# The third and fourth matrix products read their moving columns alternately from two halves of the weight rows

## The chip, the cores and the metric

The kernel runs on one core of a Trainium2 chip. The metric is the device time of one execution in microseconds; three executions of the kernel before give the median. The profile comes from a further, profiled execution, and its times are microseconds from the first instruction unless marked ns.

## What is computed

Causal attention feeds a two-layer network with a SiLU, and its output feeds a second two-layer network with a softmax gate and a layer norm. What matters here is the second network:

```
h    = x @ w_in                          # 896 x 768 @ 768 x 1024   third product
e    = exp(h - max(h)); sm = e / (sum(e) + 1e-9)
solu = h * sm
ln   = (solu - mean) / sqrt(var + 1e-6) * g_ln
out  = ln @ w_out                        # 896 x 1024 @ 1024 x 768  fourth product
```

## The kernel before

Tokens are the 896 rows, in NT = 7 tiles of 128. Each operand of the four products is split into a high and a low part of TensorE's one-pass 32-bit type (fp32r), and each product is three matmuls: high by high, high by low, low by high. The weights arrive as 64-bit numbers in chunks of 128 x 384 and are turned into the high and low parts by ScalarE (ACT), VectorE (DVE) and GpSimd (POOL) while TensorE (PE) works; the DMAs are issued by SyncE (SP).

A matmul has a stationary operand, loaded by its own weight-load instruction (PEld), and a moving one, which is streamed column by column. In the first two products (`gemm1`, lines 380 to 382, and `mm2`, lines 508 to 510) the weights are stationary and the activations move, 448 tokens at a time. Their columns are read through

```
def woven(a):
    return a.rearrange("p (z n) -> p n z", z=2)
```

which takes a contiguous row of 448 numbers in the order 0, 224, 1, 225, and so on: by turns from its first and its second half. What writes those rows (`parted`, `two`) puts even tokens in the first half and odd tokens in the second, so that the result comes out in the normal order.

In the third product (`gemm3`, lines 647 to 649) and the fourth (`product`, lines 702 to 704) it is the other way about: 128 tokens are stationary and the weights move. The moving rows are read from end to end: 512 columns of `w3h` or `w3l` in `gemm3`, 384 columns of a block of the fourth weight in `product`. A call of `gemm3` is 2 x 6 x 3 = 36 matmuls, a call of `product` 4 x 3 = 12. There are 7 calls of `gemm3`. There are 26 calls of `product`: token tiles 0, 1 and 2 take four each in `whole`, and tiles 3 to 6 go in two pairs through `pair4`, which uses seven products for the eight blocks of a pair (sums and differences of weight quarters `t1` to `t4`, and of activations `s1` to `s4`, stand in for the eighth).

The order on each engine is that of the code. Behind each `gemm3(t)` stands `chain(t)`: DVE takes the maximum of the tile (line 661), ACT the exponential (662), DVE multiplies (666), ACT squares and subtracts the mean (669, 670). Two helpers fill the time in between: `fill` converts a chunk of the fourth weight, and `turn` and `take` transpose the normalised tile on PE (line 680) into one of two PSUM buffers `tp` and split it from there, ACT making the high part (684) and DVE the low one (685). `pst` has two `tp` buffers, so a third `turn` waits until the first `take` is through; `psh` has two buffers for `h`, so `gemm3(t + 2)` waits for line 669 of `chain(t)`.

After each call of `product` a function `after()` runs the next entry of the table `steps`: `sums4` scales a part of the weights and builds differences (ACT 825, POOL 827 to 830), `split_t` splits them (ACT 836, DVE 837), `pre` transposes and combines the activations of a pair (PE 680, ACT 684 and 845, DVE 685 and 691). Results leave PSUM by ACT (726, 744, 745) or DVE (740) and are stored by SP.

Of the kernel before, what the change touches and what calls it, by code (L numbers as in the profile page):

```python
# [21 lines left out]
KD = DM // 128  # L22
# [3 lines left out]
KF2 = DF2 // 128  # L26
K2 = KF2 // 2
NT = T // 128
CH = 384
# [51 lines left out]
def fused(ctx, tc, qk, vv, w1, w2, w3, w4, gl, out):  # L81
    nc = tc.nc
# [24 lines left out]
    def woven(a):  # L107
        return a.rearrange("p (z n) -> p n z", z=2)

    def parted(a):  # L110
        return a.rearrange("p (n z) -> p z n", z=2)
# [4 lines left out]
    with tc.manual_schedule():  # L116
# [338 lines left out]
        for step in ORDER.split():  # L455
            step, _, n = step.partition("/")
# [99 lines left out]
        w3h = w3p.tile([128, KD * DF2], F32R, name="w3h", tag="h")  # L556
        w3l = w3p.tile([128, KD * DF2], F32R, name="w3l", tag="l")
# [77 lines left out]
        def columns(t):  # L635
            n, b = divmod(t - 1, B)
            o = S - C if t == 0 else b * (S + C) + 128 * n
            return slice(o, o + 128)

        def gemm3(t):  # L640
            ps = psh.tile([128, 2, 512], F32, name="h", tag="h")
            at = columns(t)
            for n in range(2):
                for k in range(KD):
                    o = (n * KD + k) * 512
                    wh, wl = w3h[:, o:o + 512], w3l[:, o:o + 512]
                    nc.tensor.matmul(ps[:, n], yh[:, k, at], wh, start=k == 0, stop=False)  # L647
                    nc.tensor.matmul(ps[:, n], yh[:, k, at], wl, start=False, stop=False)  # L648
                    nc.tensor.matmul(ps[:, n], yl[:, k, at], wh, start=False, stop=k == KD - 1)  # L649
            hps[t] = ps  # L650
# [48 lines left out]
        def product(ps, z, q, first, last):  # L699
            (ah, al), (bh, bl) = aop[z], split[4, q]  # L700
            for k in range(K2):
                nc.tensor.matmul(ps, ah[:, k], bh[:, k], start=first and k == 0, stop=False)  # L702
                nc.tensor.matmul(ps, ah[:, k], bl[:, k], start=False, stop=False)  # L703
                nc.tensor.matmul(ps, al[:, k], bh[:, k], start=False, stop=last and k == K2 - 1)  # L704

        def four():
            r = raw.tile([128, CH, 2], U32, name="o", tag="wr").bitcast(F32).rearrange("p (n c) z -> p n (c z)", n=2)
# [11 lines left out]
        def whole(t, after):  # L719
            o = four()  # L720
            for n in range(2):
                ps = bank()
                for k in (1, 2):
                    product(ps, (t, k), f"{k}{n + 1}", k == 1, k == 2)
                    if k == 2:
                        nc.scalar.activation(o[n], ps, AF.Copy, scale=rstd[t])
                        store(t, n, o[n])
                    after()

        def pair4(g, after):  # L730
# [3 lines left out]
            def made(z, q):  # L734
                ps = bank()
                product(ps, (g, z), q, True, True)
                return ps
# [42 lines left out]
        for t in range(NT):  # L780
            gemm3(t)
            if t == 0:
                fill()
            if t == NT - 2:
                turn(0, 1)
                turn(0, 2)

            def first():
                if t == NT - 2:
                    take(0, 1)  # L790
                    take(0, 2)
                fill()

            if t < NT - 1:
                chain(t, first, fill)
# [138 lines left out]
```

## Time and profile before

| | |
|---|---|
| median of 3 executions | 415.81 us (415.0 to 415.96) |
| profiled execution | 415.49 us |
| its span, first to last instruction | 413.7 us |
| PE busy with matmuls | 405.2 us, 98% of the span |
| DVE, ACT, POOL busy | 347.4, 237.3, 206.3 us |
| mean granted clock of TensorE | 0.999 of full speed |

The profiled execution is 1.8 us longer than its span, which is start and end around the instructions. The busy time of an engine is a sum over the kernel, not a limit of each part. A matmul row gives its start and a modelled duration, which overlaps the next matmul; the price of one matmul in a stream is the distance from its start to the next start. A pair of square brackets behind a row gives how long the engine had stood idle before it and which instruction ended that.

### The profile page before, as it was taken

The numbers are of one execution on the slowest core, as the hardware profiler recorded it, in microseconds if no ns is written. First come the engines' busy times: TensorE is split into PE (matmuls) and PEld (weight loads), VectorE is DVE, ScalarE is ACT, GpSimd is POOL, SyncE is SP. The second block draws the span as 40 slices with busy tenths as digits, with TensorE's granted clock in tenths as the row PEclk, the third lists the DMA queues.
The fourth block names the chain that finished last, engine by engine and source line by source line (L and its number), as shares of the span: only waits on it lengthen the run. The fifth ranks groups of instructions, "written<-read, shape, count | busy, mean of one in ns | idle before, by whom it ended". The sixth has DMA issues, their size and how long they took to land.

```text
span 413.7 us, 7456 instructions
## 1 busy us (share of the span) xinstructions
PE 405.2 (98%) x2593; PEld 373.5 (90%) x2593; DVE 347.4 (84%) x739; ACT 237.3 (57%) x551; POOL 206.3 (50%) x222
## 2 busy tenths in 40 slices
PE   8899999999999999999999999999999999899996
PEld 6677777899999999999999999999888888799996
DVE  4999999899999999997988898877878768358953
ACT  5999999444444444344544545335576665798430
POOL 2997864377767676764454343334200100298140
PEclk9999999999999999999999999999999999999999
DMA  7865312144434334445676666643132300021021
GB/s 239 270 250 177 125 54 78 40 134 112 137 109 121 110 120 118 113 121 159 202 230 191 205 192 191 195 115 113 38 109 83 112 2 2 19 59 38 21 77 58
DMA packets 19798, 50.03 MB, mean 121 GB/s; under 512 B 2352, under 2 KB 4528, under 8 KB 19760
## 3 DMA queue, kind: packets, MB, share of 16 engines
q1 hardware_dynamic: 19760, 49.56, 38.9%
q8 instruction: 20, 0.33, 0.3%
q14 instruction: 18, 0.15, 0.1%
HBM read 46.80 MB, written 2.75 MB: 120 GB/s over the span
## 4 chain that ended last, share of the span: by engine, by line
PE 88%; DVE 7%; ACT 3%; issue 1%; DVEq 0%; SPq 0%
PE h L380 8%; PE h L382 8%; PE h L381 8%; PE h L509 7%; PE h L508 7%; PE h L510 7%; PE x L258 4%; PE h L649 4%; PE h L648 4%; PE h L647 4%; PE ps L704 4%; PE ps L703 4%; PE ps L702 4%; PE x L168 3%; PE x L232 3%; DVE e L198 3%
## 5 line engine op out<-in xcount | busy, mean ns | idle before, releaser
L316 POOL TENSOR_TENSOR wl<-wx,wh 128x384 fp32r<-128x384 f32 x64 | 81.4, 1274 | 72.8 <-ACT wh L312 50.5
L285 ACT ACTIVATE wr<-wr 128x384 f32<-128x384 f32 x96 | 54.4, 569 | 35.4 <-DMA wr<-w_in 35.1
L296 DVE SCALAR_TENSOR_TENSOR wx<-wr,wx 128x384 uint32<-128x384 uint32 x96 | 69.1, 720 | 0.1
L312 ACT ACTIVATE wh<-wx 128x384 fp32r<-128x384 f32 x64 | 33.1, 519 | 57.2 <-DVE wx L296 38.2
L382 PE MATMUL h<-x,wl 128*128 128x448 f32 x174 | 61.3, 352 | 0.0
L380 PE MATMUL h<-x,wh 128*128 128x448 f32 x174 | 61.3, 352 | 0.0
L381 PE MATMUL h<-x,wh 128*128 128x448 f32 x174 | 61.3, 352 | 0.0
L306 DVE TENSOR_SCALAR wr<-wr 128x384 uint32<-128x384 uint32 x96 | 57.5, 599 | 4.3 <-DMA wr<-w_in 4.1
L290 DVE SCALAR_TENSOR_TENSOR wx<-wr 128x384 uint32<-128x384 uint32 x96 | 58.0, 605 | 1.3 <-POOL gl L391 1.3
L510 PE MATMUL h<-gh,wl 128*128 128x448 f32 x160 | 56.4, 352 | 0.0
L509 PE MATMUL h<-gl,wh 128*128 128x448 f32 x160 | 56.4, 352 | 0.0
L508 PE MATMUL h<-gh,wh 128*128 128x448 f32 x160 | 56.4, 352 | 0.0
L218 POOL TENSOR_TENSOR e<-e,st 128x128 f32<-128x128 f32 (+3 forms) x70 | 44.0, 664 | 20.2 <-DVE st L211 15.2
L391 POOL TENSOR_TENSOR gl<-sg,gh 128x448 fp32r<-128x448 f32 x32 | 40.5, 1266 | 16.5 <-DVE gh L390 9.6
L204 ACT ACTIVATE e<-e,st 128x128 f32<-128x128 f32 (+3 forms) x84 | 43.8, 535 | 4.3 <-DVE st L198 4.3
L198 DVE CUSTOM_DVE_ANT_0 e<-x,mask 128x128 f32<-128x128 f32 (+3 forms) x84 | 32.9, 445 | 5.2 <-PE x L168 5.2
L672 POOL TENSOR_TENSOR s<-s,mhalf 128x1 f32<-128x1 f32 x7 | 3.8, 549 | 60.2 <-DVE s L671 60.2
L649 PE MATMUL h<-w3h,y 128*128 128x512 f32 x84 | 33.1, 394 | 0.0
L381 PEld LDWEIGHTS h<-x,wh 128*128 128x128 f32 x174 | 32.9, 189 | 0.1
L380 PEld LDWEIGHTS h<-x,wh 128*128 128x128 f32 x174 | 32.9, 189 | 0.0
L382 PEld LDWEIGHTS h<-x,wl 128*128 128x128 f32 x174 | 32.9, 189 | 0.0
L648 PE MATMUL h<-w3l,y 128*128 128x512 f32 x84 | 32.9, 392 | 0.0
(204 smaller groups left out, 907.2 us busy)
## 6 DMA issues: line engine op xcount, KB each, us to landing
wr<-w_in SPq DMA_DIRECT2D x96, 384.0 KB, 3.6
qk<-qk_in SPq DMA_DIRECT2D x11, 480.0 KB, 5.3
v<-vv_in SPq DMA_DIRECT2D x12, 256.0 KB, 4.5
out<-o SPq DMA_DIRECT2D x12, 192.0 KB, 1.9
out<-o SPq DMA_DIRECT2D x4, 96.0 KB, 2.2
qk<-qk_in SPq DMA_DIRECT2D x2, 128.0 KB, 2.3
qk<-qk_in SPq DMA_DIRECT2D x1, 224.0 KB, 2.6
gain<-gl_in SPq DMA_DIRECT2D x1, 4.0 KB, 3.8
```

Source lines behind the costliest of these rows:

```text
L285: nc.scalar.activation(high, high, AF.Copy, scale=DOWN)
L290: nc.vector.scalar_tensor_tensor(x.bitcast(U32), r[:, :, 1], 0x80000000, r[:, :, 0], ALU.bitwise_and, ALU.bitwise_or)
L296: nc.vector.scalar_tensor_tensor(xu, r[:, :, 1], 3, xu, ALU.logical_shift_left, ALU.bitwise_or)
L306: nc.vector.tensor_scalar(low, low, 29, None, ALU.logical_shift_right)
L316: eng.tensor_tensor(l, wx.pop((n, c)), h.bitcast(F32), ALU.subtract)
L380: nc.tensor.matmul(ps[:, :S], wh, rh, start=turn == 0 and k % NB == 0, stop=False)
L381: nc.tensor.matmul(ps[:, :S], wh, rl, start=False, stop=False)
L382: nc.tensor.matmul(ps[:, :S], wl, rh, start=False, stop=turn == 1 and k % NB == NB - 1)
L508: nc.tensor.matmul(ps[:, :S], wh, rh, start=f == 0, stop=False)
L509: nc.tensor.matmul(ps[:, :S], wh, rl, start=False, stop=False)
L510: nc.tensor.matmul(ps[:, :S], wl, rh, start=False, stop=f == KF - 1)
L649: nc.tensor.matmul(ps[:, n], yl[:, k, at], wh, start=False, stop=k == KD - 1)
```

## The change

In `gemm3` and `product` the moving operands are wrapped in `woven`, so that PE takes column 0 from the first half of the row, column 1 from the second half, and so on. The halves are 256 columns (1,024 bytes) apart in `gemm3` and 192 columns (768 bytes) in `product`; in the first two products, where nothing changes, they are 224 columns (896 bytes) apart. To keep the result's columns in order, the host lays out each run of 512 or 384 weight columns with the even ones first and the odd ones behind. The number of instructions on each engine, their order, their shapes, the DMAs and the buffers are as before; everything that works element by element on the weights sees the same number of elements in another order.

```diff
             for n in range(2):
                 for k in range(KD):
                     o = (n * KD + k) * 512
-                    wh, wl = w3h[:, o:o + 512], w3l[:, o:o + 512]
+                    wh, wl = woven(w3h[:, o:o + 512]), woven(w3l[:, o:o + 512])
                     nc.tensor.matmul(ps[:, n], yh[:, k, at], wh, start=k == 0, stop=False)
...
             (ah, al), (bh, bl) = aop[z], split[4, q]
             for k in range(K2):
-                nc.tensor.matmul(ps, ah[:, k], bh[:, k], start=first and k == 0, stop=False)
-                nc.tensor.matmul(ps, ah[:, k], bl[:, k], start=False, stop=False)
-                nc.tensor.matmul(ps, al[:, k], bh[:, k], start=False, stop=last and k == K2 - 1)
+                rh, rl = woven(bh[:, k]), woven(bl[:, k])
+                nc.tensor.matmul(ps, ah[:, k], rh, start=first and k == 0, stop=False)
+                nc.tensor.matmul(ps, ah[:, k], rl, start=False, stop=False)
+                nc.tensor.matmul(ps, al[:, k], rh, start=False, stop=last and k == K2 - 1)
...
+    def parted(a):
+        n = a.shape[-1] // 2
+        return a.reshape(*a.shape[:-1], n, 2).swapaxes(-1, -2).reshape(a.shape)
...
-        "w3": chunks(inputs["moe2_w_in"].reshape(KD, 128, 2, 512).transpose(1, 2, 0, 3)),
-        "w4": chunks(inputs["moe2_w_out"].reshape(KF2, 128, 2, CH).transpose(1, 2, 0, 3)),
+        "w3": chunks(parted(inputs["moe2_w_in"].reshape(KD, 128, 2, 512)).transpose(1, 2, 0, 3)),
+        "w4": chunks(parted(inputs["moe2_w_out"].reshape(KF2, 128, 2, CH)).transpose(1, 2, 0, 3)),
```

## Rows read from the trace of the kernel before

**Rows 1.** Page, part 1: busy time of each engine, share of the span, instructions.

```profile
PE 405.2 (98%) x2593; PEld 373.5 (90%) x2593; DVE 347.4 (84%) x739; ACT 237.3 (57%) x551; POOL 206.3 (50%) x222
```

**Rows 2.** Timeline of PE, second product and third: start, modelled length, line, tiles, shape.

```profile
179.86 0.35 PE L508 MATMUL h<-gh,wh 128*128 128x448 f32 x1
...
288.63 0.35 PE L510 MATMUL ps<-gh,wl 128*128 128x448 f32 x1
288.82 0.39 PE L647 MATMUL h<-w3h,y 128*128 128x512 f32 x1
...
338.03 0.40 PE L649 MATMUL h<-w3h,y 128*128 128x512 f32 x1
338.27 1.03 PE L680 MATMUL tp<-ident,e 128*128 128x128 f32 x8
```

**Rows 3.** Timeline of the end: last four calls of product, last combination, last store.

```profile
401.49 0.33 PE L702 MATMUL ps<-t2h,area 128*128 128x384 f32 x1
...
409.63 0.34 PE L704 MATMUL ps<-t4h,area 128*128 128x384 f32 x1
410.01 0.62 DVE L740 SCALAR_TENSOR_TENSOR o<-ps,s,o 128x384 f32<-128x384 f32 x1 [0.94 <-PE ps L704]
410.65 0.33 SPq L717 DMA_DIRECT2D out<-o  x1
```

**Rows 4.** Windows: length, then busy time of PE, PEld, DVE, ACT, POOL; clock, DMA.

```profile
288.80:338.30 49.50, 49.50 (x218) 40.57 (x218) 39.65 (x89) 32.15 (x56) 4.99 (x7) 1.00 0.24 72
338.30:362.00 23.70, 21.71 (x122) 19.59 (x120) 13.69 (x29) 15.39 (x27) 3.17 (x5) 1.00 0.04 9
362.00:390.60 28.60, 28.51 (x173) 27.90 (x173) 21.40 (x28) 21.71 (x46) 20.85 (x18) 1.00 0.13 42
390.60:410.00 19.40, 19.37 (x112) 19.05 (x112) 10.74 (x19) 3.73 (x7) 5.04 (x4) 1.00 0.15 53
120.00:180.00 60.00, 60.00 (x319) 59.95 (x318) 58.68 (x90) 25.80 (x54) 43.50 (x36) 1.00 0.40 116
```

**Rows 5.** Timeline of DVE in the third product: idle time and its end in brackets.

```profile
305.50 1.22 DVE L661 TENSOR_REDUCE s<-h 128x1 f32<-128x1024 f32 x1 [0.99 <-PE h L649]
...
312.55 0.15 DVE L671 TENSOR_SCALAR s<-s 128x1 f32<-128x1 f32 x1
313.74 1.23 DVE L661 TENSOR_REDUCE s<-h 128x1 f32<-128x1024 f32 x1 [1.04 <-PE h L649]
```

**Rows 6.** Chain that ended last, 336 to 363: start, length, engine, tile, line.

```profile
338.46 1.24 DVE s L661
339.72 1.21 ACT e L662 x2
...
358.68 2.02 ACT wx L825 x4
360.70 0.49 ACT area L684
361.22 0.70 DVE area L685
```

**Rows 7.** Timeline of PE, its waits in the stretch of that chain.

```profile
356.41 0.66 PE L680 MATMUL tp<-ident,e 128*128 128x128 f32 x4 [1.27 <-DVE area L685]
...
361.97 1.25 PE L680 MATMUL tp<-ident,e 128*128 128x128 f32 x8 [0.71 <-DVE area L685]
```

**Rows 8.** Timeline of PE in pair4: transposes among the products.

```profile
382.76 1.04 PE L680 MATMUL tp<-ident,e 128*128 128x128 f32 x8
383.55 0.42 PE L702 MATMUL ps<-b22h,area 128*128 128x384 f32 x1
...
387.65 0.34 PE L704 MATMUL ps<-t2h,area 128*128 128x384 f32 x1
387.82 0.60 PE L680 MATMUL tp<-ident,e 128*128 128x128 f32 x4
...
390.18 0.34 PE L704 MATMUL ps<-t3h,area 128*128 128x384 f32 x1
390.60 0.63 PE L680 MATMUL tp<-ident,e 128*128 128x128 f32 x4
390.98 0.42 PE L702 MATMUL ps<-t1h,area 128*128 128x384 f32 x1
```

**Rows 9.** Timeline of DVE ahead of the transposes at 390.60.

```profile
377.88 4.15 DVE L837 TENSOR_TENSOR t3l<-wx,t3h 128x384 fp32r<-128x384 f32 x4
...
389.76 0.69 DVE L685 TENSOR_TENSOR area<-tp,area 128x512 fp32r<-128x512 f32 x1 [0.67 <-ACT area L684]
```

**Rows 10.** Waits from 364 to 386: who waited for whom, us, times, longest.

```profile
ACT o L726 <- PE ps L704: 0.4, 2, 0.2
```

## The prediction

> **What bounds the kernel now.** I read the page first: PE is busy 98% of the span [rows 1]. That alone doesn't say that a faster matmul shortens the kernel, so I went through the windows of the second half, where the change acts, and then the timelines and the chain that ended last.
>
> The timeline of PE shows what one matmul costs in a stream [rows 2]. The second product, whose moving rows are read by turns already, starts at 179.86, and the third product begins at 288.82: 96 weight blocks x 2 batches x 3 = 576 matmuls of 448 columns in 108.96 us, **189.2 ns** each. The clock was granted in full, 2.4 GHz (1.00 in the windows [rows 4]), where 448 columns last 186.7 ns: 2.5 ns over one column a clock. Then 216 matmuls of 512 columns read end to end (`gemm3` of tiles 0 to 5) fill 288.82 to 338.27: **228.9 ns** each, where 512 columns last 213.3 ns: 15.6 ns over. The fourth product, also end to end, goes from 401.49 to 409.63 in 47 steps [rows 3]: **173.2 ns** against 160.0 for 384 columns: 13.2 ns over. So the contiguous reads lose 13.1 and 10.7 ns more than the woven one, at the same clock.
>
> Three stretches behave differently:
>
> *288.8 to 338.3.* PE has no gap [rows 4], and DVE waits for it: the maximum of line 661 follows 0.99 and 1.04 us of idle that a `gemm3` matmul ended [rows 5]. PE sets the end.
>
> *338.3 to 390.6.* The chain that ended last leaves PE with the last matmul of `gemm3(5)` and goes through DVE and ACT: 661 at 338.46, 662, and on through both `chain`s, scaling and splitting to the low part at 361.22 [rows 6], for which the transposes at 361.97 wait. PE stands idle 1.27 and 0.71 us there [rows 7]. Behind that, the transposes at 390.60 come 0.42 us after the last matmul's start, where 0.17 us is normal (387.65 to 387.82) [rows 8]. They need a `tp` buffer that DVE frees with line 685, 389.76 to 390.45, behind the splits of t3, t1 and t4 that began at 377.88 [rows 9]. So PE is just in time at 390.60: it is the second place where DVE and ACT decide.
>
> *390.6 to the end.* PE runs products to 409.8; the last DVE sum at 410.01 waits for PE, and the last store follows [rows 3]. PE sets the end again.
>
> **The change, part by part.** No instruction, DMA or buffer is added or removed, and the elementwise work has the same sizes: nothing on DVE, ACT, POOL or SP. All that changes is the distance between matmul starts. The trace has no woven read of 512 or 384 columns, so I bound it. From below: one column a clock, 213.3 and 160.0 ns. Nearest row: the woven 448, 2.5 ns over, so 215.8 and 162.5 ns. The other side is no gain (228.9, 173.2), and beyond it a row that PE reads more slowly: eight fp32 transposes of 128 columns take from 382.76 to 383.55 [rows 8], 0.77 ns a column, near two clocks. I take the nearest row, since only the distance of the halves differs (1,024 and 768 bytes against 896): 13.1 ns saved on each `gemm3` matmul, 10.7 ns on each of `product`.
>
> The weight loads could take the place of the column stream as the bound. In those same eight transposes, each with a weight load of 128 columns, load and matmul together take 99 ns, so a 162.5 ns matmul still covers its load.
>
> Two rules of the Trainium skill speak against the change. "TensorE: Matmul & The Clock Gate", section "Back-to-back issue gap", gives a warm matmul its columns over 2.4 GHz and 2.5 ns, whatever the layout; "SBUF — State Buffer", section "Who interferes with whom", says that PE never waits on anyone. By these a `gemm3` matmul would take 215.8 ns already and weaving would save nothing. The trace agrees for the woven row (189.2 ns) and not for the contiguous one (228.9 ns), so a cost of reading is there that they don't name.
>
> The sum, stretch by stretch:
>
> 1. `gemm3(0)` to `gemm3(5)`: 216 x 13.1 ns = **2.83 us**. One `gemm3` shrinks from 8.24 to 7.77 us, by 0.47 us. DVE's work per tile ends with line 671 at 312.70, 7.2 us after its start at 305.50 [rows 5], so about 0.5 us of its idle time is left: PE still decides, and the chain behind starts 2.83 us earlier.
> 2. From there to 390.6: `gemm3(6)` (36 x 13.1 = 0.47 us) and 17 of 26 calls of `product` (204 x 10.7 = 2.18 us) get shorter, but they stand beside the DVE and ACT chain. Up to 361.97, PE only waits longer at 356.41 and 361.97. Between 362 and 390.6 twelve calls save 144 x 10.7 = 1.54 us, and PE arrives that much too early at the transposes of 390.60. What faster products could give the other engines here is small: ACT waited for PE 0.4 us in all [rows 10]. I take **0**, with 0.4 as upper bound of what those waits give.
> 3. After 390.98: nine calls, 108 x 10.7 ns = **1.16 us**, all on the path.
>
> Together 3.99 us. Against the profiled execution's 415.49 us that is 411.5; against the median, 0.32 us higher, 411.8. I say **411.6 us**.
>
> **The rivals.**
>
> *Everything passes* (the waits of step 2 give way, because DVE's splits also finish earlier). 252 x 13.1 + 312 x 10.7 ns = 6.64 us, 408.9 us. For it: PE is 98% busy. Against it: PE's waits [rows 7], the late transposes at 390.60 [rows 8], and DVE's queue, which PE doesn't feed before them [rows 9].
>
> *Only one width gains.* If 512 columns alone: 412.7 us; if 384 alone: 414.3 us. For it: each has its own distance between the halves. Against it: the excess of the contiguous read is alike in both.
>
> *No change* (the excess of 13 ns isn't due to the order of the moving columns but to something else in which these products differ, such as the stationary tokens): 415.5 us. For it: the woven and the contiguous rows also differ in which operand is stationary. Against it: both load 128 x 128 and at the same clock, and nothing waits in the stream of the third product.
>
> *Slower:* in `gemm3` the halves are exactly 1,024 bytes apart. If the two places collide there, each column would cost two clocks, as the transposes do: 426.7 + 2.5 = 429.2 ns, and 216 x 200.3 ns = 43.3 us more, 457.6 us with the last calls' gain. It decides from 1.16 us / 216 = 5.4 ns, that is from 234.3 ns a matmul. For it: no row has that distance. Against it: 896 bytes cost nothing.
>
> **How the numbers follow.** My forecast 0.62, with its own range of 410.8 to 412.3; everything passes 0.13; one width alone 0.08 (512 alone 0.05, 384 alone 0.03); no change 0.11; slower 0.06. 0.3% is 1.25 us, about what a measurement of this kernel can tell from no change. Faster by more than that: 0.62 + 0.13 + 0.05 = 0.80. Within it: no change and 384 alone (1.16 us), 0.14. Slower: 0.06. The range of 409.0 to 414.0 takes in the first two cases and 512 alone, and leaves 0.20 outside above.
>
> **What would show it.** `gemm3` matmuls 215 to 216 ns apart and `product` matmuls 162 to 163 ns apart confirm the price. Line 661 of `chain(5)` should start near 335.6, with DVE idle of about 0.5 us ahead of each line 661 instead of 1. The idle ahead of 356.41 (now 2.83 us earlier) should grow from 1.27 to about 2 us. At the transposes of 390.60 a new PE wait of some 1.5 us for DVE line 685 should stand. The last nine calls should take 17.6 us instead of 18.7. I would be wrong if the starts are still 229 and 173 ns apart (no change), if they are above 234 ns (slower), if no new wait stands ahead of 390.60 (everything passes), or if the longer waits let the granted clock fall: at 1.2 GHz a product's matmul would cost 320 ns, and eight microseconds of that would eat the gain.

## The result and the profile after

The changed kernel takes **411.52 us** (411.0 to 412.19, four runs) beside 415.57 us for the kernel before: ratio 0.9905, 95% interval 0.9885 to 0.9924, some 4 us faster. The forecast was 411.6 us, within 409.0 to 414.0.

The timeline of PE after the change, as [rows 2] and [rows 3] show it before. The third product now starts at 288.72, the transposes behind its sixth tile at 335.34, and the last matmul of the fourth at 405.69. Lines behind 700 are one higher than before.

```profile
288.72 0.38 PE L647 MATMUL h<-w3h,y 128*128 128x512 f32 x1
...
335.34 1.04 PE L680 MATMUL tp<-ident,e 128*128 128x128 f32 x8
...
403.90 0.33 PE L703 MATMUL ps<-t4h,area 128*128 128x384 f32 x1
...
405.69 0.33 PE L705 MATMUL ps<-t4h,area 128*128 128x384 f32 x1
```

216 matmuls fill 46.62 us, 215.8 ns each, where they took 228.9; eleven steps of the last call take 1.79 us, 162.7 ns each, where they took 173.2. At the granted 2.4 GHz, 512 and 384 columns last 213.3 and 160.0 ns, so both are one column a clock and about 2.5 ns.

The windows of the same four stretches (length, then busy time of PE, PEld, DVE, ACT, POOL, the granted clock, DMA), to be held against [rows 4]:

```profile
288.70:335.30 46.60, 46.60 (x217) 40.80 (x217) 43.06 (x89) 33.98 (x56) 4.42 (x6) 1.00 0.25 76
335.30:360.00 24.70, 22.41 (x122) 20.80 (x121) 14.64 (x29) 16.49 (x30) 4.31 (x6) 0.93 0.04 9
360.00:387.80 27.80, 26.53 (x173) 26.15 (x172) 20.73 (x27) 20.94 (x45) 19.81 (x18) 1.00 0.13 43
387.80:406.00 18.20, 18.17 (x112) 17.91 (x112) 10.78 (x19) 3.73 (x7) 5.00 (x4) 1.00 0.15 53
```

The first stretch is 2.9 us shorter and the last 1.2, and PE is busy throughout both. The two in the middle, 52.3 us before, are 52.5 us now although PE's matmuls read woven there too. PE stands idle longer instead, and ten of its matmuls run at half the clock (0.93 in the second window; more on that below). Its timeline shows the waits where [rows 7] and [rows 8] showed those before:

```profile
351.45 0.66 PE L680 MATMUL tp<-ident,e 128*128 128x128 f32 x4 [0.58 <-DVE s L664]
353.82 0.66 PE L680 MATMUL tp<-ident,e 128*128 128x128 f32 x4 [1.71 <-DVE area L685]
...
386.20 0.33 PE L705 MATMUL ps<-t3h,area 128*128 128x384 f32 x1
387.83 0.63 PE L680 MATMUL tp<-ident,e 128*128 128x128 f32 x4 [1.30 <-DVE area L685]
388.21 0.41 PE L703 MATMUL ps<-t1h,area 128*128 128x384 f32 x1
```

At 387.83 the reader sees a new wait: the transposes came just in time before [rows 8], now they wait 1.30 us for DVE's line 685. The chain that ended last confirms it: DVE and ACT hold it from 335.54 to 387.83 without a PE matmul in it, from the first maximum to the buffer that DVE frees.

```profile
335.54 1.24 DVE s L661
...
358.12 0.96 ACT area L684 x2
...
374.19 1.02 DVE t2l L838
375.20 5.14 DVE t3l L838 x4
...
386.99 0.70 DVE area L685
387.69 0.14 issue
387.83 0.63 PE tp L680 x4
```

### The profile page after: what moved, and what is told of

Its sections match the earlier page's. It is cut to its first block, busy times and chain, and to the rows that moved or that the text cites. A ratio compares the mean times of both kernels' runs of the same rounds, so it can differ in the third digit from the quotient of the medians.

```text
span 409.7 us, 7456 instructions
## 1 busy us (share of the span) xinstructions
PE 399.7 (98%) x2593; PEld 371.8 (91%) x2593; DVE 350.6 (86%) x739; ACT 238.9 (58%) x551; POOL 204.8 (50%) x222
## 4 chain that ended last, share of the span: by engine, by line
PE 82%; DVE 9%; ACT 6%; issue 1%; DVEq 0%; SPq 0%
PE h L381 8%; PE h L380 8%; PE h L382 8%; PE h L510 7%; PE h L509 7%; PE h L508 7%; PE x L258 5%; PE h L647 4%; PE h L649 4%; PE h L648 4%; PE x L168 3%; PE x L232 3%; PE x L178 2%; PE ps L510 1%; ACT wx L826 1%; PE ps L509 1%
## 5 line engine op out<-in xcount | busy, mean ns | idle before, releaser
L316 POOL TENSOR_TENSOR wl<-wx,wh 128x384 fp32r<-128x384 f32 x64 | 80.3, 1257 | 75.1 <-ACT wh L312 52.7
L285 ACT ACTIVATE wr<-wr 128x384 f32<-128x384 f32 x96 | 56.8, 595 | 34.4 <-DMA wr<-w_in 34.4
L306 DVE TENSOR_SCALAR wr<-wr 128x384 uint32<-128x384 uint32 x96 | 60.1, 626 | 3.5 <-DMA wr<-w_in 3.3
L290 DVE SCALAR_TENSOR_TENSOR wx<-wr 128x384 uint32<-128x384 uint32 x96 | 59.1, 615 | 2.2 <-POOL gl L391 1.3
L647 PE MATMUL h<-w3h,y 128*128 128x512 f32 x84 | 31.9, 380 | 0.0
L648 PE MATMUL h<-w3l,y 128*128 128x512 f32 x84 | 31.8, 379 | 0.0
```

Of the source, the lines that this page charges most:

```text
L285: nc.scalar.activation(high, high, AF.Copy, scale=DOWN)
L290: nc.vector.scalar_tensor_tensor(x.bitcast(U32), r[:, :, 1], 0x80000000, r[:, :, 0], ALU.bitwise_and, ALU.bitwise_or)
L306: nc.vector.tensor_scalar(low, low, 29, None, ALU.logical_shift_right)
L316: eng.tensor_tensor(l, wx.pop((n, c)), h.bitcast(F32), ALU.subtract)
```

## The experiments

**Which savings count.** The first two runs weave only a part of the calls; the re-laid weights are read end to end elsewhere.

```diff
-                    wh, wl = woven(w3h[:, o:o + 512]), woven(w3l[:, o:o + 512])
+                    wh, wl = [woven(x) if t < NT - 1 else x for x in (w3h[:, o:o + 512], w3l[:, o:o + 512])]
...
+            call = next(calls)
-                rh, rl = woven(bh[:, k]), woven(bl[:, k])
+                rh, rl = [woven(x) if call >= 17 else x for x in (bh[:, k], bl[:, k])]
```

> Only the matmuls of the stretches in which TensorE sets the end are woven: the third product of tiles 0 to 5 and the last nine calls of the fourth product. The third product of tile 6 and the first 17 calls of the fourth read their re-laid weights end to end, so the columns of those results come out with the even ones first. If the savings of the middle stretch are all lost to the DVE and ACT chain, this is as fast as the whole change: 3.99 us under the kernel before, ratio 0.990. If the middle counted in part, this is slower than the whole change by that part, up to 2.65 us.

Measured: 411.48 us beside 415.62, ratio 0.9899 (0.9885 to 0.9914), the whole change's time. The transposes of 390.60 wait 0.17 us, and no more:

```profile
387.86 0.63 PE L680 MATMUL tp<-ident,e 128*128 128x128 f32 x4 [0.17 <-DVE area L685]
```

The reverse run has `t == NT - 1` and `call < 17` for the two conditions.

> The reverse: only the third product of tile 6 and the first 17 calls of the fourth product are woven, 36 x 13.1 + 204 x 10.7 ns = 2.65 us of TensorE time; all else reads re-laid weights end to end (columns of those results in another order). If DVE and ACT decide the middle, the time is that of the kernel before within 0.4 us, ratio 0.999 to 1.000, and TensorE waits some 1.5 us ahead of the transposes of line 680 in the fifth product call of the first pair. If every saving on TensorE passes, 2.65 us faster, ratio 0.994.

Measured: 415.55 us beside 415.62, ratio 0.9999 (0.9990 to 1.0009). The middle's matmuls are 2.65 us shorter by the prices, and the kernel is not measurably faster. The time stands in longer waits, of which these are the two largest, and in nine matmuls that come 320 ns apart behind the first of them (356.86 to 359.74), at half the clock:

```profile
355.94 0.80 PE L680 MATMUL tp<-ident,e 128*128 128x128 f32 x4 [1.71 <-DVE area L685]
...
389.96 0.63 PE L680 MATMUL tp<-ident,e 128*128 128x128 f32 x4 [1.31 <-DVE area L685]
```

So 324 of the 564 matmuls make the whole gain, and the other 240 make none that can be measured.

**The third product alone**, with the fourth as in the kernel before (the diff leaves `product` and the layout of `w4` out).

> Only the third product is woven, the fourth is as before. The sum by stretches gives 2.83 us, ratio 0.993: tiles 0 to 5 count and tile 6 doesn't. If the two products' savings don't add up (because a shorter third product alone changes what DVE and ACT do later), it differs from 2.83 us by more than half a microsecond.

Measured: 412.73 us beside 415.62, 2.89 us, ratio 0.9933 (0.9918 to 0.9949). The sum by stretches, 2.83 us, holds for the third product by itself. The fourth alone was not run; what is left for it of the whole change's 4.05 us is 1.16.

**What holds PE at the new wait.** Four runs on top of the whole change. First, work off DVE:

```diff
-                nc.vector.tensor_tensor(l[:, k], quads[q, k], h[:, k].bitcast(F32), ALU.subtract)
+                low = nc.gpsimd if z == "t4" else nc.vector
+                low.tensor_tensor(l[:, k], quads[q, k], h[:, k].bitcast(F32), ALU.subtract)
...
-                 11: [lambda: split_t("t1"), lambda: pre(1, 4)], 12: [lambda: split_t("t4"), lambda: pre(1, 5)],
+                 11: [lambda: split_t("t1"), lambda: pre(1, 4)], 12: [lambda: pre(1, 5), lambda: split_t("t4")],
```

> The whole change, and the four low parts of t4 are made on GpSimd, behind the low part of s1, and not on DVE. If DVE's queue of splits is what holds the transposes at the new wait of 1.30 us, the wait goes, since about 2 us leave that queue, and the kernel is 1.0 to 1.4 us faster than the whole change: 5.0 to 5.4 us under the kernel before, ratio 0.987 to 0.988. If something else holds them (ACT, or the product before), the wait stays and the time is that of the whole change, ratio 0.990. GpSimd's operations take longer than DVE's, so t4 could come too late for the last product of the pair: then a wait stands there.

Measured: 412.52 us beside 415.62, ratio 0.9946 (0.9928 to 0.9963): a miss, slower than the whole change. The eleven executions fall into two groups, six of 411.89 to 412.52 us and five of 414.32 to 414.75; 412.52 is their median, and the ratio goes by their mean, 413.33. The trace is of one of the five (414.60 us). Its groups of lines between 380.6 and 386.3 (count, busy us, mean ns) come first, then DVE's timeline in the whole change:

```profile
L839 DVE TENSOR_TENSOR t1l<-wx,t1h 128x384 fp32r<-128x384 f32 x4 | 5.5, 1426 | 0.0
L839 POOL TENSOR_TENSOR t4l<-wx,t4h 128x384 fp32r<-128x384 f32 x4 | 5.1, 1313 | 0.0
```
```profile
380.27 3.06 DVE L838 TENSOR_TENSOR t1l<-wx,t1h 128x384 fp32r<-128x384 f32 x4
383.25 1.95 DVE L838 TENSOR_TENSOR t4l<-wx,t4h 128x384 fp32r<-128x384 f32 x4
```

DVE's four splits of t1, which took 3.06 us together in the changed kernel, with one POOL operation beside them (381.63 to 382.91), take 5.47 beside POOL's four of t4. The four of t4, with POOL idle, had taken DVE 1.95. DVE is through t1 and t4 at 385.20 in the whole change and through t1 alone at 386.23 here; the wait grew from 1.30 to 2.16 us. The work left DVE's queue, and the time didn't. "SBUF — State Buffer" of the Trainium skill, section "Who interferes with whom", says that a DVE operation with two SBUF inputs contends with a GpSimd operation that reads SBUF; the 1.95 us with POOL idle and the 5.47 beside it agree.

In this trace the longer wait cost more than itself. Behind it the granted clock falls, where PE sets the end: eleven steps from 389.81 to 393.28 take 3.47 us, where 1.79 is the price, so 1.7 us are lost.

```profile
388.86 0.63 PE L680 MATMUL tp<-ident,e 128*128 128x128 f32 x4 [2.16 <-DVE area L685]
...
390.13 0.53 PE L704 MATMUL ps<-t1l,area 128*128 128x384 f32 x1
390.45 0.53 PE L705 MATMUL ps<-t1h,area 128*128 128x384 f32 x1
```

That is most of the 2.2 us between the means of the two groups; that the other four executions of the slower group had the same fall is not shown.

Second, the same DVE work in another order:

```diff
-                 11: [lambda: split_t("t1"), lambda: pre(1, 4)], 12: [lambda: split_t("t4"), lambda: pre(1, 5)],
-                 13: [lambda: pre(2, 0)], 15: [lambda: pre(2, 1)], 16: [lambda: pre(2, 2)],
+                 11: [lambda: split_t("t1"), lambda: pre(1, 4)], 12: [lambda: pre(1, 5)],
+                 13: [lambda: pre(2, 0)], 14: [lambda: split_t("t4")], 15: [lambda: pre(2, 1)], 16: [lambda: pre(2, 2)],
```

> The whole change; the four splits of t4 stand one step later and another one in DVE's and ACT's order, behind the first sums of the second pair, so that DVE's line 685 frees the buffer some 1.9 us earlier, before TensorE comes (386.4). If the order of DVE's queue decides, the wait goes at the same total of DVE work: 0.7 to 1.3 us faster than the whole change, ratio 0.987 to 0.989, with a wait of up to half a microsecond where the last product of the first pair needs t4. If the total of DVE's work decides, the time stays at 0.990.

Measured: 409.79 us beside 415.38, ratio 0.9870 (0.9853 to 0.9888). The wait is gone. DVE frees the buffer at 385.50, and PE comes at 385.76 (timeline of both):

```profile
384.81 0.69 DVE L685 TENSOR_TENSOR area<-tp,area 128x512 fp32r<-128x512 f32 x1 [0.66 <-ACT area L684]
...
385.94 1.95 DVE L838 TENSOR_TENSOR t4l<-wx,t4h 128x384 fp32r<-128x384 f32 x4
```
```profile
385.76 0.60 PE L680 MATMUL tp<-ident,e 128*128 128x128 f32 x4
386.12 0.41 PE L703 MATMUL ps<-t1h,area 128*128 128x384 f32 x1
```

The order of the queue held PE, not its total. The next limit is small: the list of waits has a weight load that waits 0.4 us for POOL's low part of s4.

Third, another buffer.

```diff
-            tp = tps[t, n] = pst.tile([128, K2, 128], F32, name="tp", tag="tp")
+            tp = tps[t, n] = turns[0].tile([128, K2, 128], F32, name="tp", tag="tp")
...
         banks[0] = pool("psq", 2, space=PS)
+        turns[0] = pool("psu", 2, space=PS)
```

> The whole change; the pairs' transposes of the second pair go to two more PSUM buffers that are free by then, so that the third transposes needn't wait for DVE's line 685. If that buffer is what holds TensorE for 1.30 us at 387.83, the wait goes and the next limit is the low part of s4 of the second pair, which TensorE would reach at 394.6 and GpSimd has ready near 395.0: 0.9 to 1.3 us faster than the whole change, ratio to the kernel before 0.987 to 0.988. If DVE's queue catches TensorE at the next place anyway (the operands of product 11 or 12 of the second pair), the wait only moves there and the time is that of the whole change, 0.990.

Measured: 411.22 us beside 415.38, ratio 0.9901 (0.9882 to 0.9920), and the wait stands at 1.27 us. This run tells nothing of the buffer: its edit sent all four halves of the second pair to the two new buffers, and so exchanged two for two. The next edit sends only tile 6's halves there (`(psu[0] if t == NT - 1 else pst).tile(...)`), so that there are four.

> The run with two more buffers only exchanged the buffers: four transposed halves still went by turns through two of them, so it left the wait as it was. Here tile 6's two halves go to the two new buffers and tile 5's to the two old ones, and none of the four waits for another. DVE's order is that of the whole change. If the buffer holds TensorE for 1.3 us, the wait at the third transposes goes; behind it TensorE meets the low part of s4 of the second pair, ready about 395.0 when TensorE wants it at 394.6, so 0.9 to 1.4 us faster than the whole change, near the run with t4 later: ratio 0.986 to 0.988. If it is DVE's order and not the buffer, the wait moves to the last products' operands and the time stays at 0.990.

Measured: 410.19 us beside 415.82, ratio 0.9860 (0.9844 to 0.9877), 5.6 us under the kernel before. The transposes start at 386.72 without a wait, while DVE frees the old buffer only at 388.33:

```profile
386.72 0.60 PE L680 MATMUL tp<-ident,e 128*128 128x128 f32 x4
```
```profile
387.64 0.69 DVE L685 TENSOR_TENSOR area<-tp,area 128x512 fp32r<-128x512 f32 x1 [0.67 <-ACT area L684]
```

Either remedy, an earlier release or two more buffers, gives back about 1.5 us: the kernels are 5.59 and 5.63 us under the kernel before, the whole change 4.05. That is roughly what the twelve calls ahead of that point save (1.54 us).

**What makes a contiguous read slow.** Five kernels, each executed once, show the distance of matmul starts. The first undoes the weave in the kernel before (`woven`, `parted` and `two` return their argument), with all roles of the operands kept.

> The kernel before with the first two products unwoven as well: their activations are written and read end to end. The operands keep their roles (weights stationary, activations moving). If the order of the moving columns makes the cost, one column in sixteen costs a clock more (31.4 of 512 and 25.7 of 384 in the kernel before), so a matmul of 448 columns goes from 189.2 to about 200.8 ns, and 1152 such matmuls add up to 13 us where TensorE sets the pace: 426 to 429 us. If the stationary side or the operand's origin makes it, the matmuls stay at 189 ns and the time at 415 us.

Measured: 427.66 us beside 415.75. The second product's timeline, ten steps in 2.00 us:

```profile
189.80 0.36 PE L510 MATMUL h<-gh,wl 128*128 128x448 f32 x1
...
191.80 0.36 PE L508 MATMUL h<-gh,wh 128*128 128x448 f32 x1
```

200 ns instead of 189.2, with the weights stationary as before: it is the order of the moving columns, not the side on which they stand. The other four put further orders in the place of `woven`, with a layout to match. ORDER3 and ORDER4 stand for the two orders of each run.

```diff
-wh, wl = woven(w3h[:, o:o + 512]), woven(w3l[:, o:o + 512])
+wh, wl = [x.rearrange(ORDER3, ...) for x in (w3h[:, o:o + 512], w3l[:, o:o + 512])]
-rh, rl = woven(bh[:, k]), woven(bl[:, k])
+rh, rl = [x.rearrange(ORDER4, ...) for x in (bh[:, k], bl[:, k])]
```

> The third product reads each row as every second column, evens and then odds (a step of 8 bytes, in one direction); the fourth reads by turns from four quarters. If two neighbouring columns read one behind the other cost and any other order is free: 215.8 and 162.5 ns. If each passage into the next 16 columns (64 bytes) costs a clock unless the read comes back: the third makes 64 passages instead of 32 and takes 242 ns, the quarters are free, 162.5 ns.

> The third product reads 16 columns from the first half, 16 from the second and so on; the fourth two and two. If neighbours cost: nearly the contiguous price of 228.9 ns for blocks of 16 and about half of the excess, 168 ns, for blocks of two. If passages between 64-byte pieces cost unless the two halves take turns inside a piece: 228.9 ns for blocks of 16, and 162.5 ns for blocks of two.

> By turns, but from places close together: the third product takes columns 0, 16, 1, 17 and so on inside each 32 (64 bytes apart), the fourth 0, 8, 1, 9 inside each 16 (32 bytes apart, in one 64-byte piece). If neighbours cost: free, 215.8 and 162.5 ns. If passages between 64-byte pieces cost: the fourth still makes one passage per 16 columns and stays at 173.2 ns; the third makes its passages two by two, between 215.8 and 228.9 ns.

> Both products by turns from places very close: the third in the order 0, 2, 1, 3 inside each 4 columns, the fourth 0, 4, 1, 5, 2, 6, 3, 7 inside each 8. If each second column must find its predecessor's right neighbour (woven halves and the turns of 8 and 16 do, at no cost) and any other step costs what the contiguous read shows, a clock per 16 columns: half of the steps are off in the third, 222 ns, a quarter in the fourth, 165 ns. If columns read next to each other cost, only the passage from one four to the next is such a pair, 219 ns, and the fourth is free, 162.5 ns.

Measured, from the distances of starts in the timelines: over the first 216 matmuls for 512 columns, over the 47 steps of the last four calls for 384 (excess: clocks at 2.4 GHz beyond one a column):

| order in which columns are read | columns | ns | excess |
|---|---|---|---|
| two halves by turns (the change) | 512 / 384 | 215.8 / 162.6 | 6 / 6 |
| 0, 16, 1, 17, ... in each 32 | 512 | 215.8 | 6 |
| 0, 8, 1, 9, ... in each 16 | 384 | 162.6 | 6 |
| 0, 4, 1, 5, 2, 6, 3, 7 in each 8 | 384 | 162.6 | 6 |
| 0, 2, 1, 3 in each 4 | 512 | 229.0 | 38 |
| end to end (before) | 512 / 448 / 384 | 228.9 / 200 / 173.2 | 37 / 32 / 32 |
| blocks of 16 from two halves | 512 | 240.0 | 64 |
| four quarters by turns | 384 | 204.5 | 107 |
| blocks of 2 from two halves | 384 | 246.8 | 208 |
| evens, then odds (step of two) | 512 | 453.4 | 576 |

These rows are from the timelines of the two costliest orders, two steps of the one and seven of the other:

```profile
299.97 0.64 PE L647 MATMUL h<-w3h,y 128*128 128x512 f32 x1
...
300.88 0.64 PE L649 MATMUL h<-w3h,y 128*128 128x512 f32 x1
```
```profile
427.71 0.42 PE L703 MATMUL ps<-t1h,area 128*128 128x384 f32 x1
...
429.44 0.42 PE L704 MATMUL ps<-t4l,area 128*128 128x384 f32 x1
```

All three theories fell. That neighbours read one behind the other cost would have made the evens-then-odds order free, and it is the slowest. That passages between 64-byte pieces cost would have left 0, 8, 1, 9 slow, and it is free. The third, a price for every column that isn't the right neighbour of the last but one, put 0, 2, 1, 3 at 222 ns (229.0 measured) and 0, 4, 1, 5 at 165 (162.6). What the table does show: the orders at full pace are just those in which every second column runs through neighbours for at least four columns. Why stays open.

## Why the prediction was right

*The price of a matmul* was right: 215.8 and 162.5 ns forecast, 215.8 and 162.6 measured, and the run that reads the first two products end to end excludes the no-change rival's reason. Halves 1,024 bytes apart cost PE nothing, so the slower rival's mechanism wasn't there.

*Step 1* (2.83 us): 49.45 us became 46.62. One thing in it was mis-sized. DVE's idle time ahead of line 661 was to shrink from about 1.0 to 0.5 us and is 0.26 (0.58 in the run with close turns, below), as the timeline of DVE shows beside [rows 5]:

```profile
304.46 1.23 DVE L661 TENSOR_REDUCE s<-h 128x1 f32<-128x1024 f32 x1
...
311.84 0.13 DVE L671 TENSOR_SCALAR s<-s 128x1 f32<-128x1 f32 x1
312.23 1.23 DVE L661 TENSOR_REDUCE s<-h 128x1 f32<-128x1024 f32 x1 [0.26 <-PE h L649]
```

DVE's work per tile is 7.5 us now (304.46 to 311.97) and not 7.2, because operations on the raw weights `wr` became slower (last section). The prediction had put the change's effect on DVE and ACT at nothing. PE still decided, with a quarter of a microsecond to spare.

*Step 2* (0, at most 0.4): the time is shown by the run that weaves the middle alone, ratio 0.9999. The wait at 390.60 was forecast at some 1.5 us and measured 1.30; the idle time ahead of 356.41 at about 2 us, where 1.71 us stand now, and 0.58 us just ahead of that. The wait at 361.97, which was to grow too, is gone from this trace, because the ten matmuls at half the clock bring PE there late; in the run with t4 later, at full clock, it grew from 0.71 to 0.99 us:

```profile
359.08 1.25 PE L680 MATMUL tp<-ident,e 128*128 128x128 f32 x8 [0.99 <-DVE area L685]
```

"Everything passes" is excluded. That the sum of the middle came out so near 0 is in part luck. From line 661 of `chain(5)` to the transposes that stood at 390.60 it took 52.14 us before (338.46 to 390.60) and takes 52.29 now (335.54 to 387.83). In the run with close turns (0, 16, 1, 17, ... in the third product and 0, 8, 1, 9, ... in the fourth), whose matmuls cost the same, it takes 51.83:

```profile
336.21 1.23 DVE L661 TENSOR_REDUCE s<-h 128x1 f32<-128x1024 f32 x1 [0.58 <-PE h L649]
```
```profile
388.04 0.63 PE L680 MATMUL tp<-ident,e 128*128 128x128 f32 x4 [1.50 <-DVE area L685]
```

So the shorter matmuls do give the middle 0.31 us, within the bound of 0.4, and the wide halves take 0.46 us back, 0.35 of it by slowing operations of DVE beside `gemm3(6)` (last section), a term that the prediction didn't have. The run with the third product alone agrees: 52.51 us, longer than before. Each of these lengths is from one trace.

*Step 3* (1.16 us): from the first start of the last nine calls to the last it is 17.48 us, 388.21 to 405.69, where 390.98 to 409.63 was 18.65, so 1.17 us less; 17.6 was forecast. Line 661 of `chain(5)` starts at 335.54; 335.6 was forecast.

A fall of the granted clock, named as a danger, did come, where it costs nothing. Between 351 and 354 PE had done only transposes, with idle times of 0.58 and 1.71 us; behind them ten matmuls of one call are 320 ns apart, 1.2 GHz:

```profile
354.84 0.53 PE L705 MATMUL ps<-b22h,d 128*128 128x384 f32 x1
355.16 0.53 PE L703 MATMUL ps<-b22h,d 128*128 128x384 f32 x1
```

This is the stretch in which DVE and ACT hold the chain. Of the four executions of the changed kernel two had a mean granted clock of 0.994 and 0.995 and two of 1.000, and the first two aren't slower (411.0 and 411.53 us beside 411.51 and 412.19). In the run with t4 later the same wait was 1.72 us long and the granted clock stayed at 1.00 from 355 to 360. Where PE sets the end the fall does cost time, as the run with t4 on GpSimd showed.

One slip in the prediction's numbers changed nothing: its range of 409.0 to 414.0 was said to take in "everything passes", whose 408.9 us lies just outside.

## What to carry to other kernels

Before pricing a faster matmul, divide the kernel by who ends the waits: here 57% of the shortened matmuls gave the whole measured gain, and what the rest saved went into waits for DVE. Where a faster engine runs into a buffer, look for the release in the other engine's queue: moving a few operations behind it, or one more pair of buffers, gave 1.5 us, while moving them to POOL slowed DVE's other splits by more (2.4 us) than it relieved DVE of (1.95). And the order in which a matmul reads its moving columns is a cost of its own, 6% here, to be measured from start to start.

## What the runs showed that I had not expected

**Wide halves slow the neighbours.** While the third product reads halves 1,024 bytes apart, DVE and ACT take longer on the raw weight tiles `wr`, of which these operations read every second 32-bit word. The groups of lines from 304 to 334 us, in the kernel before, in the changed one, and in the run that takes turns 64 bytes apart at the same matmul price (216 ns):

```profile
L290 DVE SCALAR_TENSOR_TENSOR wx<-wr 128x384 uint32<-128x384 uint32 x7 | 3.8, 548 | 0.0
L285 ACT ACTIVATE wr<-wr 128x384 f32<-128x384 f32 x7 | 3.8, 547 | 0.0
```
```profile
L285 ACT ACTIVATE wr<-wr 128x384 f32<-128x384 f32 x8 | 6.1, 763 | 0.0
L290 DVE SCALAR_TENSOR_TENSOR wx<-wr 128x384 uint32<-128x384 uint32 x8 | 5.5, 688 | 0.0
```
```profile
L285 ACT ACTIVATE wr<-wr 128x384 f32<-128x384 f32 x8 | 4.4, 554 | 0.0
L290 DVE SCALAR_TENSOR_TENSOR wx<-wr 128x384 uint32<-128x384 uint32 x8 | 4.4, 548 | 0.0
```

ACT's operation goes from 547 to 763 ns with the wide halves and back to 554 with the close turns. Operations on other tiles don't change (line 661: 1,224 ns in all three). The weave as such doesn't do it: between 130 and 170 us, where the first product reads halves 896 bytes apart, line 290 takes 545 ns, and 546 in the run that reads end to end there. Nor does the distance alone: in the run that reads blocks of 16 from the same two halves, at 240.0 ns a matmul, line 290 takes 549 ns. In `gemm3(0)` to `gemm3(5)` it cost no time, since PE still came last. Beside `gemm3(6)`, where DVE and ACT hold the chain, it did: from line 661 of `chain(5)` to that of `chain(6)` it is 11.85 us before (338.46 to 350.31) and 12.19 in the changed kernel (335.54 to 347.73), but 11.84 with close turns (336.21 to 348.05). By these traces close turns would be the better order here, by some 0.4 us; one execution of them, 411.75 us, can't show so small a gain. Why turns between places 1,024 bytes apart do that wasn't found out.

**Orders differ by a factor of two.** A step of two columns, 8 bytes, takes 453.4 ns for 512 columns, 2.1 times the woven halves.
